# Attention phases of a fused attention and gated-MLP kernel placed one slot later against their start, with hand-set starts in the first block

## The chip, the cores and the metric

The kernel runs on 1 core of a Trainium2 chip. The metric is the device time of one execution in microseconds (us), median of three runs. The span in the profile is the part between the first and the last instruction.

## The reference

Three stages follow each other. The first is a gated linear attention with a 48x48 state for each of 32 heads (4 batches, 8 heads), over 768 positions; the second multiplies two projections and projects back; the third does the same with `h - tanh(h)`.

```python
f = 1.0 / (1.0 + np.exp(-f_logit))
for t in range(S):
    state = f[:, :, t, :, None] * state + np.einsum('bhd,bhe->bhde', k[:, :, t], v[:, :, t])
    y[:, :, t] = np.einsum('bhd,bhde->bhe', q[:, :, t], state)
...
x = ((x @ w_a) * (x @ w_b)) @ w_out        # 3072 x 384, d_ff 1536
h = x @ w_in                               # d_ff2 2048
return (h - np.tanh(h)) @ w_out2
```

## The kernel before

The order of all work is written out by hand; each engine executes its own queue in that order.

**Attention.** The sequence is cut into 12 chunks of 64 positions; with two halves of the batch this makes 24 steps. A step is a generator (`attn_step`) of twelve phases, named by the letters `FPRKVSMUYELD`: F sigmoid on ScalarE; P and R the forward and backward scans on VectorE; K three multiplies on VectorE that make KH, RA and RB (`L305` to `L307`); V two state copies on ScalarE; S the scores (`sc`) and transposes (`pk`) on TensorE; M the score evacuations RA, RB and KTS on ScalarE, with the causal masks on GpSimd; U the state update matmuls (`uu`) on TensorE, their sum T on VectorE (`L347`) and a multiply on GpSimd; Y the output matmuls (`yy`); E and L their evacuation to x on ScalarE and VectorE; D, in the last step of a block, six small transfers x<-y that complete x. Four steps make a block of 512 tokens; the kernel has 6 blocks. S needs the step's RA and RB, U needs KTS, and Y needs the first half of T, because its PSUM bank is the one that `uu` left.

**First MLP.** `moe1` runs 12 values of m over each block, three slots for each: after the `a` group of 9 matmuls and its ScalarE copy `asb` the first slot, after the `b` group, the VectorE product `gf` and its split the second, after the `y` group of the m before it the third. So slot s has `a` at s mod 3 = 0, `b` at 1 and `y` at 2, and a block has 36 slots. `gf` and `asb` have one buffer, and the `b` bank is free for the next m when `gf` has read it. While block jb is multiplied, the steps of block jb+1 are woven in: a table `OFF` and `LEAD` give each phase the slot behind which it is issued (`pulses`). All steps of blocks 1 to 5 use one working set, and the loads of the next step are issued at F and Y.

**Weight conversion.** The weights lie in HBM as 64-bit numbers. `w_tick` converts one 128x384 tile: three VectorE instructions (`L124` to `L126`), then a ScalarE copy and a GpSimd (later VectorE) subtraction (`L136`, `L138`). In the first block every slot 0 to 32 has one conversion, issued before that slot's phases, and the tile is used by the matmul group four slots later. Its input lies in three staging buffers `wst`, loaded from the sync queue. From block 1 on two conversions in nine slots prepare the third stage's weights (`CONV`), spilled to HBM.

**Second MLP.** From about 640 us `h` and `o` matmuls run with no attention beside them.

Of the kernel before, what the change touches and what calls it, by code (L numbers as in the profile page):

```python
# [28 lines left out]
def tile_kernel(ctx: ExitStack, tc: tile.TileContext, q, k, v, f, w_a, w_b, w_out, w_in, w_out2, l_fkq, l_tv, l_v, l_w1, l_w2, out):  # L29
# [16 lines left out]
    NSTEP = 2 * NC  # L46
    blocks = [4, 4, 4, 4, 4, 4]
    NBLK = len(blocks)
    first = [sum(blocks[:j]) for j in range(NBLK)]
    block_of = [j for j, n in enumerate(blocks) for _ in range(n)]  # L50
    PRO = blocks[0]
    SLOTS = 3 * MF
    LEAD = 6
    PHASES = "FPRKVSMUYELD"
    OFF = (0, 1, 2, 4, 5, 6, 6, 8, 9, 9, 10, 11)
    CONV = (3, 7)
    SEQ = ("lf0 lk0 lf1 lt0 lk1 lv0 lf2 lt1 lv1 lk2 w lf3 lt2 lv2 lk3 w lt3 lv3 w x x x x F0 P0 F1 R0 K0 x x lf4 lk4 x V0 S0 P1 M0 F2 "
           "R1 K1 U0 Y0 lt4 lv4 x V1 S1 P2 E0 F3 M1 R2 L0 K2 x U1 Y1 x V2 S2 P3 E1 M2 L1 R3 K3 x U2 Y2 x V3 S3 x x E2 M3 c L2 F4 c P4 "
           "x x U3 x Y3 x E3 L3 R4 c K4 V4")
    TW = 528  # L60

    const = ctx.enter_context(tc.tile_pool(name="const", bufs=1))
# [79 lines left out]
    def w_spill():  # L142
        name, m, wt = spilled.pop(0)
        nc.sync.dma_start(out=wsp[2 * m + "ip".index(name)], in_=wt.bitcast(F32))
# [21 lines left out]
    with tc.manual_schedule(), ExitStack() as p1:  # L166
# [64 lines left out]
        def t_of(i):  # L231
            return T[i if i < min(PRO, 4) else i % 2]

        def tv_of(i):
            return TV[i if i < min(PRO, 4) else i % 2]
# [4 lines left out]
        def load_t(i, sl):  # L240
            t = t_of(i)
            if i < PRO:
                nc.sync.dma_start(out=t[:, sl], in_=l_fkq[i, :, sl])
            else:
                for r0 in (0, 64):
                    nc.sync.dma_start(out=t[r0:r0 + D, sl], in_=l_fkq[i, r0:r0 + D, sl])

        def load_v(i):
            w = w_of(i)
            for ab, (vs, r0) in enumerate(((w.VS_A, 64), (w.VS_B, 0))):  # L250
                nc.sync.dma_start(out=vs[r0:r0 + 64], in_=l_v[i, ab])

        def load_tv(i):
            nc.sync.dma_start(out=tv_of(i), in_=l_tv[i])
# [21 lines left out]
        Y3 = {}  # L276
# [121 lines left out]
        pulses = []  # L398
        for jb in range(1, NBLK):
            for si in range(blocks[jb]):  # L400
                for p, o in enumerate(OFF):
                    at = (9 * si + o) * SLOTS // (9 * blocks[jb]) - LEAD
                    pulses.append((SLOTS * (jb - 1) + at, first[jb] + si, p))
        pulses.sort(key=lambda e: e[0])

        phase = [0] * NSTEP
# [1 line left out]
        def pulse(i, p):  # L408
            assert phase[i] == p
            phase[i] += 1  # L410
            if i >= PRO and p == 0 and i + 1 < NSTEP:
                load_t(i + 1, slice(0, 3))
                load_tv(i + 1)
            next(gens[i], None)
            if i >= PRO and PHASES[p] == "Y" and i + 1 < NSTEP:
                load_v(i + 1)
# [11 lines left out]
        def w_tick(upto):  # L428
            while nconv[0] < upto and (loaded or half):
                if loaded:  # L430
                    half.append(w_start(loaded.pop(0)))
                    w_fetch()
                if len(half) > 1 or not loaded or half[0][0] in "abo":
                    w_finish(half.pop(0))
                nconv[0] += 1
# [70 lines left out]
        for it in SEQ.split():  # L506
            if it == "c":
                w_tick(nconv[0] + 1)
            elif it == "w":
                w_fetch(len(loaded) + 1)  # L510
            elif it == "x":
                warm()
            elif it[0] == "l":
                i = int(it[2])
                if it[1] == "f":
                    load_t(i, slice(0, 1))
                elif it[1] == "k":
                    load_t(i, slice(1, 3))
                else:
                    (load_tv if it[1] == "t" else load_v)(i)  # L520
            else:
                i, p = int(it[1]), PHASES.index(it[0])
                if i >= PRO:
                    pulses.pop(0)
                pulse(i, p)
        for i in range(PRO):
            pulse(i, len(PHASES) - 1)
# [14 lines left out]
        for g, jb in enumerate(moe1(None)):  # L542
            slot = g % SLOTS
            if jb == 0:
                w_tick(min(NW1, npro + slot + 1))
            else:
                if g == SLOTS:
                    rot.update(n=3, conv=None)
                if spilled:
                    w_spill()  # L550
                if (g + LEAD) % (SLOTS // 4) in CONV and jb < NBLK - 1 or (jb == NBLK - 1 and slot == 0):
                    w_tick(min(nconv[0] + 1, NW2 + 1))
            while pulses and pulses[0][0] <= g:
                _, i, p = pulses.pop(0)
                pulse(i, p)
            if not pulses and not done:
                done = True
                nc.vector.tensor_reduce(r1, PMS.rearrange("p i u -> p (i u)"), mybir.AxisListType.X, ALU.min)
                nc.vector.tensor_scalar(r1, r1, P_MIN, None, ALU.is_ge)
            if jb == NBLK - 1:  # L560
                if slot == 2:
                    x2first.append(load_x2(0))
                elif slot > 2 and fills and len(fills) > 2 * MF2 + 3 - slot:
                    w_fill(*fills.pop(0))
# [37 lines left out]
        for i in range(NO * MF2 + LAG):  # L602
            g = None
            if i < NO * MF2:
                o, m = divmod(i, MF2)
# [196 lines left out]
```

## Time and profile before

| what | value |
|---|---|
| median of 3 runs | 997.63 us (997.12 to 998.8) |
| profiled execution | 997.97 us, span 996.3 us |
| TensorE (matmul) busy | 961.1 us, 96% of the span |
| VectorE, ScalarE, GpSimd busy | 620.4, 475.1, 123.3 us |
| mean granted TensorE clock | 0.983 |

The busy shares are averages over three regimes: the first some 40 us with four steps of attention alone, the first block with its conversions (to about 155 us), and the rest. The profiled execution lies 1.7 us above its own span, and 0.3 us above the median.

### The profile page before, as it was taken

The numbers are of one execution on the slowest core, as the hardware profiler recorded it, in microseconds if no ns is written. First come the engines' busy times: TensorE is split into PE (matmuls) and PEld (weight loads), VectorE is DVE, ScalarE is ACT, GpSimd is POOL, SyncE is SP. The second block draws the span as 40 slices with busy tenths as digits, with TensorE's granted clock in tenths as the row PEclk, the third lists the DMA queues.
The fourth block names the chain that finished last, engine by engine and source line by source line (L and its number), as shares of the span: only waits on it lengthen the run. The fifth ranks groups of instructions, "written<-read, shape, count | busy, mean of one in ns | idle before, by whom it ended". The sixth has DMA issues, their size and how long they took to land.

```text
span 996.3 us, 15895 instructions
## 1 busy us (share of the span) xinstructions
PE 961.1 (96%) x6155; PEld 773.3 (78%) x6155; DVE 620.4 (62%) x1045; ACT 475.1 (48%) x925; POOL 123.3 (12%) x144
## 2 busy tenths in 40 slices
PE   7879989999999999999999999999999999999997
PEld 4667767887887788887888888888888888888885
DVE  8787875666656566675552238666666666666663
ACT  4424443333433433343422137666666666666663
POOL 5456552000110010000100000000000000000000
PEclk9889989999999999999999999999999999999999
DMA  9456654545634554564228651020100100200001
GB/s 276 111 154 170 170 136 135 142 114 131 186 106 114 142 175 125 128 194 121 85 75 325 195 184 47 1 96 1 63 33 1 64 33 1 95 1 1 32 1 35
DMA packets 41172, 104.54 MB, mean 105 GB/s; under 512 B 5600, under 2 KB 8672, under 8 KB 41088
## 3 DMA queue, kind: packets, MB, share of 16 engines
q1 hardware_dynamic: 40368, 102.45, 34.8%
q10 hardware_dynamic: 720, 0.98, 0.5%
q8 instruction: 50, 0.82, 0.4%
q14 instruction: 34, 0.28, 0.1%
HBM read 74.71 MB, written 26.74 MB: 102 GB/s over the span
## 4 chain that ended last, share of the span: by engine, by line
PE 89%; DVE 7%; issue 1%; DMA 1%; ACT 1%; POOL 0%; DVEq 0%; ACTq 0%
PE o L164 20%; PE h L164 20%; PE b L164 15%; PE a L164 13%; PE y L164 13%; PE yy L357 2%; PE sc L319 2%; PE pk L323 1%; PE uu L339 1%; DVE cv L125 1%; PE sc L320 1%; DVE cv L124 1%; DVE PRE L293 1%; DVE RA L306 1%; DVE R L298 1%
## 5 line engine op out<-in xcount | busy, mean ns | idle before, releaser
L164 PE MATMUL h<-x,w_i 128*128 128x512 f32 x864 | 213.0, 391 | 0.0
L164 PE MATMUL o<-gh,w_p 128*128 128x512 f32 x576 | 194.7, 393 | 0.0
L164 PEld LDWEIGHTS h<-x,w_i 128*128 128x128 f32 x864 | 162.2, 188 | 36.4
L164 PE MATMUL b<-x,w_b 128*128 128x512 f32 x648 | 169.3, 407 | 0.0
L492 DVE TENSOR_TENSOR gf<-asb,b 128x512 f32<-128x512 f32 x72 | 49.4, 686 | 192.1 <-PE b L164 128.9
L164 PE MATMUL a<-x,w_a 128*128 128x512 f32 x648 | 164.5, 398 | 2.6 <-DMA x<-y 2.3
L164 PE MATMUL y<-gh,w_o 128*128 128x512 f32 x432 | 146.1, 393 | 0.0
L164 PEld LDWEIGHTS a<-x,w_a 128*128 128x128 f32 x648 | 120.4, 189 | 31.0 <-ACT gh L493 2.7
L164 PEld LDWEIGHTS b<-x,w_b 128*128 128x128 f32 x648 | 122.9, 195 | 26.2
L104 DVE SCALAR_TENSOR_TENSOR xu<-u,h 128x512 f32<-128x512 f32 x96 | 66.0, 688 | 111.8 <-ACT u L101 111.7
L164 PEld LDWEIGHTS o<-gh,w_p 128*128 128x128 f32 x576 | 108.2, 188 | 24.7
L101 ACT ACTIVATE u<-h 128x512 f32<-128x512 f32 x96 | 57.5, 599 | 132.7 <-PE h L164 132.0
L164 PE MATMUL o<-gl,w_p 128*128 128x512 f32 x288 | 113.1, 393 | 0.0
L487 ACT ACTIVATE asb<-a 128x512 f32<-128x512 f32 x72 | 43.0, 597 | 141.0 <-PE a L164 139.1
L493 ACT ACTIVATE gh<-gf 128x512 fp32r<-128x512 f32 x72 | 45.6, 633 | 125.9 <-DVE gf L492 125.7
L164 PEld LDWEIGHTS y<-gh,w_o 128*128 128x128 f32 x432 | 81.1, 188 | 18.2
L164 PE MATMUL y<-gl,w_o 128*128 128x512 f32 x216 | 84.8, 393 | 0.0
L105 DVE SCALAR_TENSOR_TENSOR v<-v,xu 128x512 f32<-128x512 f32 x96 | 66.4, 692 | 10.4 <-ACT v L102 0.5
L106 DVE SCALAR_TENSOR_TENSOR v<-v,v 128x512 f32<-128x512 f32 x96 | 66.5, 692 | 10.0
L102 ACT ACTIVATE v<-u,bias 128x512 f32<-128x512 f32 x96 | 69.6, 725 | 3.1
L103 ACT ACTIVATE v<-u,bias 128x512 f32<-128x512 f32 x96 | 68.1, 710 | 0.6 <-DVE gl L574 0.6
L574 DVE TENSOR_TENSOR gl<-v,gh 128x512 fp32r<-128x512 f32 x96 | 65.7, 684 | 0.2 <-ACT gh L573 0.2
(96 smaller groups left out, 1119.2 us busy)
## 6 DMA issues: line engine op xcount, KB each, us to landing
wst<-in_l_w_dram SPq DMA_DIRECT2D x68, 384.0 KB, 3.3
wsp<-wst SPq DMA_DIRECT2D x32, 384.0 KB, 2.4
T<-in_l_fkq_dram SPq DMA_DIRECT2D x38, 288.0 KB, 5.2
x<-xs SPq DMA_DIRECT2D x12, 768.0 KB, 5.3
w_i<-wsp SPq DMA_DIRECT2D x16, 384.0 KB, 3.6
w_p<-wsp SPq DMA_DIRECT2D x16, 384.0 KB, 3.6
TV<-in_l_tv_dram SPq DMA_DIRECT2D x24, 192.0 KB, 5.4
xs<-oh SPq DMA_DIRECT2D x18, 256.0 KB, 2.3
```

The costliest lines, as they stand in the source:

```text
L101: nc.scalar.activation(u, h, ACTF.Square, accum_out=total)
L102: nc.scalar.activation(v1, u, ACTF.Square, bias=bias1)
L103: nc.scalar.activation(v2, u, ACTF.Square, bias=bias2)
L104: nc.vector.scalar_tensor_tensor(xu, u, Q4, h, ALU.mult, ALU.mult)
L105: nc.vector.scalar_tensor_tensor(v1, v1, Q_Y1, xu, ALU.add, ALU.mult)
L106: nc.vector.scalar_tensor_tensor(v2, v2, Q_Y2, v1, ALU.add, ALU.mult)
L164: nc.tensor.matmul(dst, l_, r_, start=(first and i == 0), stop=(last and i == 2))
L319: nc.tensor.matmul(sc[64:128, u], KH[0:64, u], RA[0:64, u], start=True, stop=True)
L487: nc.scalar.activation(asb, pb, ACTF.Copy)
L492: nc.vector.tensor_tensor(gf, asb, pab[1], ALU.mult)
L493: nc.scalar.activation(gh, gf, ACTF.Copy)
L574: nc.vector.tensor_tensor(gl, g, gh.bitcast(F32), ALU.subtract)
```

## The change

The phases S to D move one place away from F (`OFF`), and `LEAD` grows by one. For blocks 2 to 5 this leaves S to D in their slots, issues F, P, R, K and V one slot earlier, and the conversions too, which use the same `LEAD`. For the four steps of block 1, woven into the first block, a table `FIRST` gives the slot of F by hand: F moves from -6, 3, 12, 21 to -5, 4, 12, 20, so that S moves from slots 0, 9, 18, 27 to 2, 11, 19, 27, and U from 2, 11, 20, 29 to 4, 13, 21, 29. V of step 4 moves from the prologue into slot 0. The load of the next step's `TV` moves from F to K.

```diff
-    LEAD = 6
+    LEAD = 7
+    FIRST = (-5, 4, 12, 20)
     PHASES = "FPRKVSMUYELD"
-    OFF = (0, 1, 2, 4, 5, 6, 6, 8, 9, 9, 10, 11)
+    OFF = (0, 1, 2, 4, 5, 7, 7, 9, 10, 10, 11, 12)
...
-           "x x U3 x Y3 x E3 L3 R4 c K4 V4")
+           "x x U3 x Y3 x E3 L3 R4 c K4")
...
-                    at = (9 * si + o) * SLOTS // (9 * blocks[jb]) - LEAD
-                    pulses.append((SLOTS * (jb - 1) + at, first[jb] + si, p))
+                    at = FIRST[si] + o if jb == 1 else SLOTS * (jb - 1) + 9 * si - LEAD + o
+                    pulses.append((at, first[jb] + si, p))
...
                 load_t(i + 1, slice(0, 3))
+            if i >= PRO and PHASES[p] == "K" and i + 1 < NSTEP:
                 load_tv(i + 1)
```

TensorE at step 5's scores, before. The first row is `a` of m=3, `pk` ends S; rows of `sc` stand for sixteen.

```order
L164 MATMUL a<-x,w_a_886 128x512 x9
L319 MATMUL sc<-RA,KH 64x64
...
L320 MATMUL sc<-RB,KH 64x64
L323 MATMUL pk<-ident,KH 128x128 x4
L164 MATMUL b<-x,w_b_911 128x512 x9
L164 MATMUL y_867<-gh,w_o_937 128x512
```

The same place after the change, from `a` of m=3 to the first state matmul of step 5.

```order
L165 MATMUL a<-x,w_a_859 128x512 x9
L165 MATMUL b<-x,w_b_905 128x512 x9
L165 MATMUL y_840<-gh,w_o_936 128x512
...
L324 MATMUL pk<-ident,KH 128x128 x4
L165 MATMUL a<-x,w_a_955 128x512 x9
L165 MATMUL b<-x,w_b_981 128x512 x9
L340 MATMUL uu_1109<-TV_183,KTS 64x48 x2
```

The scores now stand behind `b` and `y`; `uu` stands behind a `b` group, where it stood behind a `y` group.

ScalarE at step 5's evacuations, before: the weight copies are those of slots 8 and 9.

```order
L136 ACTIVATE w_a_959<-wc 128x384
L310 ACTIVATE VS_A<-ST_131 64x8x48
L311 ACTIVATE VS_B<-ST_131 64x8x48
L487 ACTIVATE asb<-a 128x512
L136 ACTIVATE w_b_983<-wc 128x384
L327 ACTIVATE RA<-sc 64x512
L327 ACTIVATE RB<-sc 64x512
L332 ACTIVATE KTS<-pk 128x512
L493 ACTIVATE gh<-gf 128x512
```

The same place after the change; the weight copies are those of slots 10 and 11.

```order
L137 ACTIVATE w_o_1009<-wc 128x384
L137 ACTIVATE w_a_1028<-wc 128x384
L328 ACTIVATE RA<-sc 64x512
L328 ACTIVATE RB<-sc 64x512
L333 ACTIVATE KTS<-pk 128x512
L489 ACTIVATE asb<-a 128x512
L137 ACTIVATE w_b_1077<-wc 128x384
```

RA, RB and KTS now stand behind the copy of slot 11 and ahead of `asb` of m=4; before, `asb` of the running m stood ahead of them.

## Rows read from the trace of the kernel before

**Rows 1.** Busy time by stretch: us, PE, PEld, DVE, ACT, POOL, clock, DMA share, GB/s

```profile
81.00:110.00 29.00, 24.71 (x214) 19.90 (x207) 24.11 (x43) 12.09 (x24) 17.50 (x16) 0.94 0.58 159
430.00:520.00 90.00, 90.00 (x700) 72.22 (x698) 52.34 (x100) 32.79 (x64) 8.46 (x12) 1.00 0.38 114
```

**Rows 2.** Groups of VectorE instructions, 41.6 to 150.9 us; last number idle before

```profile
L492 DVE TENSOR_TENSOR gf<-asb,b 128x512 f32<-128x512 f32 x11 | 7.5, 686 | 20.4 <-PE b L164 13.2 <-POOL RA L328 5.4 <-POOL w_b L138 1.8
L293 DVE TENSOR_TENSOR_SCAN PRE<-F,D 128x520 f32<-128x520 f32 x4 | 4.9, 1232 | 0.0
L306 DVE TENSOR_TENSOR RA<-T,PRE 64x512 f32<-64x512 f32 x3 | 4.4, 1474 | 0.0
```

**Rows 3.** TensorE's waits, 0 to 160 us: total, times, longest

```profile
PE sc L319 <- DVE RA L306: 17.3, 5, 4.0
```

**Rows 4.** Timeline around the scores of step 6

```profile
101.37 0.30 PE L319 MATMUL sc<-RA,KH 64*64 64x64 f32 x2 [3.95 <-DVE RA L306]
107.33 0.69 DVE L492 TENSOR_TENSOR gf<-asb,b 128x512 f32<-128x512 f32 x1 [1.69 <-PE b L164]
107.93 0.56 DVE L124 TENSOR_SCALAR cv<-wst 128x384 int32<-128x384 int32 x1
109.78 0.56 DVE L124 TENSOR_SCALAR cv<-wst 128x384 int32<-128x384 int32 x1
111.51 0.62 DVE L347 TENSOR_TENSOR T<-uu,ST 128x192 f32<-128x192 f32 x2
```

**Rows 5.** Timeline of VectorE, first instruction of slot 0's conversion

```profile
41.58 0.56 DVE L124 TENSOR_SCALAR cv<-wst 128x384 int32<-128x384 int32 x1
```

**Rows 6.** Chain that ended last, 133 to 191 us: start, us, what

```profile
133.47 3.23 PE b L164 x9
...
150.42 0.56 DVE wc L126
...
151.07 4.35 DMA x<-y
155.55 3.54 PE a L164 x9
...
183.41 2.08 PE b L164 x9
...
187.56 0.61 PE uu L339 x32
...
190.46 1.08 PE yy L357 x32
```

**Rows 7.** Timeline of ScalarE, evacuations of step 6

```profile
105.95 0.53 ACT L136 ACTIVATE w_b<-wc 128x384 fp32r<-128x384 f32 x1
107.61 0.58 ACT L332 ACTIVATE KTS<-pk 128x512 f32<-128x512 f32 x1
112.27 0.60 ACT L487 ACTIVATE asb<-a 128x512 f32<-128x512 f32 x1
```

**Rows 8.** TensorE by stretch: us, busy, granted clock, DMA share, GB/s

```profile
50.70:52.60 1.90, 0.06 (x1) 1.00 0.57 142
55.00:57.50 2.50, 2.50 (x7) 0.54 0.71 184
```

**Rows 9.** Timeline in block 1 and at the change to block 2

```profile
228.83 0.58 ACT L332 ACTIVATE KTS<-pk 128x512 f32<-128x512 f32 x1
232.25 0.68 PE L339 MATMUL uu<-TV,KTS 64*64 64x48 f32 x32
240.06 2.19 SPq L380 DMA_DIRECT2D x<-y  x3
245.74 0.68 DVE L305 TENSOR_TENSOR KH<-T,R 128x512 f32<-128x512 f32 x1
246.68 2.22 PE L164 MATMUL a<-x,w_a 128*128 128x512 f32 x9
```

**Rows 10.** Landing of the staged weights' transfers, 40 to 150 us

```profile
DMA to landing us min/median/max: 3.0/3.2/7.0
```

## Prediction

> **What bounds the kernel now.** I read the busy table by stretch first. From 430 to 520 us TensorE is busy in all of its 90 us at a clock of 1.00 [rows 1], and it is so in every stretch from 160 us to the end of the first MLP: there the step costs what its matmuls cost, and a phase moved within a gap of another engine changes nothing. In the first block it is different: 24.71 of 29 us busy, clock 0.94, with VectorE at 24.11 of 29 [rows 1]. The waits name the place: TensorE waited five times, 17.3 us in total, at the first score matmul for VectorE's RA [rows 3].
>
> That is half of a circle. VectorE's groups show the other half: between the first and the last conversion of the block it stood idle 20.4 us, all of it in front of `gf`, waiting for the `b` group [rows 2]. One turn, at step 6: `sc` waits 3.95 us for RA and starts at 101.37; then come `sc`, `pk` and `b`, so `gf` of m=6 starts at 107.33 after 1.69 us of idling [rows 4], and the next `gf` waits again. Then VectorE works without a pause until the next RA, and TensorE waits. Whoever is late makes the other wait, alternately. (Two of the releasers in the row of `gf` are GpSimd's; what `gf` needs is `asb` and `b`, and `b` ended right before.)
>
> So I do the accounting on VectorE. Its conversion of slot 0 starts at 41.58 [rows 5], that of slot 32 ends at 150.98 (150.42 and 0.56), and the next block's first `a` starts at 155.55 [rows 6]: a stretch of 109.4 us, of which 20.4 are idle [rows 2] and 89.0 are work in queue order, and a tail of 4.6 us (ScalarE's copy, then the transfers x<-y of 4.35 us [rows 6]). The change alters none of the 89.0 except what it reorders. What it saves is what it takes out of the 20.4.
>
> **The first block after the change.** S of steps 4 and 5 stands two slots later, of step 6 one, while K of step 7 stands one slot earlier. Prices: a conversion takes VectorE 1.85 us (107.93 to 109.78), `gf` 0.60 (107.33 to 107.93), T 0.62 [rows 4], P 1.23 [rows 2]; a matmul group 2.08, `uu` 0.61, `yy` 1.08 [rows 6].
>
> Does S still wait in a way that VectorE feels? From the end of `gf` of m=2, VectorE does two conversions and K (about 6.9 us at the durations of step 6) and step 5 is ready; TensorE, from the end of that same `b`, has `y`, `a`, `b`, `y` to do, 8.3 us. As VectorE reaches that `gf` 1 to 2 us late, S waits about 1 us at most and VectorE not at all. It then stays behind TensorE, and each `gf` finds its `b` finished, with these exceptions, where something else is late:
>
> - `asb` of m=1 and m=4 now stands in ScalarE's queue behind RA, RB and KTS of steps 4 and 5, and these behind the weight copy of slots 2 and 11. From the end of that conversion the five copies take 2.9 us: copy to the end of KTS 2.24 (105.95 to 108.19) and 0.60 of `asb` [rows 7], plus 0.04. VectorE has one conversion of 1.85 meanwhile: idle 1.05 at each of two `gf`, 2.1.
> - The V copies of step 6 stand ahead of `asb` of m=6: 0.3.
> - At step 6 KTS is ready 2.28 us after the conversion of slot 19, so `uu`, now in slot 21, waits some 2 to 3 us for ScalarE. `uu` and `b` of m=7 end 4.97 after that conversion; VectorE, with two conversions, T and P, arrives after 5.5. Nothing at full clock.
> - At step 7 `uu`, `a`, `yy`, `b` of m=10 end 8.13 after the conversion of slot 27, VectorE, with `gf`, three conversions, T and P, arrives after 7.9 to 8.0: 0.2.
>
> These are 2.6 us. The clock adds to them. TensorE's idling of 1.9 us from 50.70 to 52.60 is followed by a granted clock of 0.54, the lower of its two levels (1.2 of 2.4 GHz) but for the part where it changes [rows 8], and a `b` after such a wait takes 3.23 us where others take 2.08 [rows 6]. The new waits of `uu` are 2 to 3 us long, so I count the lower clock behind each: 1.15 us more for the next group. Behind steps 4 and 5 VectorE is late enough to hide it; behind 6 and 7 it makes the two items 0.6 and 1.3. The sum is 2.1 + 0.3 + 0.6 + 1.3 = 4.3 us of idle left.
>
> One item more: R of step 8 is issued before the conversion of slot 32, which ends the stretch, where it stood behind it: about 1.6 us are added (a scan like P's 1.23 [rows 2] behind two small instructions on 8 columns, taken as 0.2 each).
>
> Saved: 20.4 - 4.3 - 1.6 = 14.5 us. Without any lower clock it would be 16.2.
>
> **What else moves, at nothing.** V of step 4 goes from the prologue to slot 0; ScalarE waits for the conversion there. The load of `TV` goes from F to K, four slots later; its reader U comes more than ten slots after. Both pass only staged weight loads on the sync queue. Those are asked for when the conversion three before has read the buffer, so with `gf` and two conversions between them they have 4.3 us, against a landing of 3.2 in the median and 7.0 at worst [rows 10]. If that cover were gone, VectorE would wait in the conversions.
>
> In blocks 2 to 5 S to D keep their slots. The conversion now stands at S, its ScalarE copy ahead of RA: 0.5 us in a queue where KTS ends at 229.41 and `uu` starts at 232.25 [rows 9], 2.8 us of cover. K stands a slot earlier, ahead of its `gf`, which comes some 1.5 us late; the `b` bank that it frees is wanted two groups, S and more later. At the change of block the transfers x<-y are issued at 240.06 and need some 4.4 us; `a` starts at 246.68 [rows 9], 2.2 us to spare, and the `T` load that stood just ahead of them now stands further ahead. So nothing there.
>
> **How fast VectorE is itself** is the term that the trace leaves open, since it will run with GpSimd for a larger share of the time. RA took 1.47 us in this stretch [rows 2], while KH, the same kind of multiply, took 0.68 in block 1, where GpSimd is nearly idle [rows 9]. If the scans and all three multiplies of each step were held as RA is, up to 0.8 each for the three that are not held now, four steps would cost 7 to 9 us; if none were held, 4 us would be gained. I take today's durations, because the multiplies still follow conversions, whose GpSimd subtractions they meet now too.
>
> The Trainium skill (SBUF — State Buffer, section "SBUF: two separate sides") says that VectorE and GpSimd share a port pair by an exclusive lock, which a VectorE instruction with two SBUF inputs takes, and that the loser waits for the whole instruction. RA's 1.47 us agrees. By that rule alone, with GpSimd busy in most of the shortened block, I would expect the held case, and about 991 us.
>
> **Forecast and rivals.** The sum stands against the profiled execution's own 997.97 (span 996.3 and 1.7 around it), 0.3 above the median: 997.97 - 14.5 = 983.5.
>
> - Likeliest, VectorE-bound first block with a few microseconds of idle left: 980 to 988, chance 0.58.
> - VectorE itself slower (multiplies and scans held, or staged loads late by a microsecond in some conversions): 14.5 less 4.5 to 12, so 988 to 995.6, about 991. For it: GpSimd has the same work in less time. Against: RA is held already [rows 2], so GpSimd's share is in today's work. 0.20.
> - More saved, no lower clock and multiplies held less: below 980. 0.08.
> - The wait moves, no gain: `uu` waits for KTS behind conversions, and `asb` behind them makes `gf` late by as much as before. This needs 4 to 5 us of idle per step; the queue from conversion to `asb` is 2.9 long, with 1.85 of VectorE's work beside it. Then 998; 0.05.
> - Slower: the conversion at S in blocks 2 to 5 makes KTS late for `uu` in each of 16 steps. An idling of 1.9 and the lower clock's 1.15 would cost 3 us a step, 48 in all, less the 14.5: about 1031. It decides when RA, RB and KTS come over 2.8 us later than now; the copy put ahead takes 0.5 and its input is ready. 0.09 for this and smaller cases of its kind.
>
> A change of 0.2% (2 us) is about what a measurement of this kernel tells from none. Faster by more: 0.58 + 0.20 + 0.08 = 0.86; within it 0.05; slower 0.09. The range leaves out no more than the slower and the unchanged cases and the edges: 980.0 to 991.5, where the held multiplies stand.
>
> **What would show it.** Right: the next block's first `a` near 141 us, VectorE's idle before `gf` near 5 us in the block, no wait of 4 us of `sc` for RA, and in its place waits of `uu` for KTS of 2 to 3 us with a lower clock behind them. Wrong: RA, RB or the scans longer than now; idle in front of the conversions for staged loads; any TensorE wait after 160 us.

## The result

The changed kernel takes 987.67 us (median of 4 runs, 986.92 to 988.12) against 997.5 us (997.12 to 998.8) for the kernel before: a ratio of 0.9902, 95% interval 0.9885 to 0.992, or 9.8 us less. The profiled execution's span went from 996.3 to 985.4 us, and the mean granted clock from 0.983 to 0.993.

All of it lies ahead of 160 us. By stretch, with the columns of [rows 1] (us, PE, PEld, DVE, ACT, POOL, clock, DMA share, GB/s), the changed kernel shows:

```profile
81.00:110.00 29.00, 25.03 (x217) 19.91 (x217) 24.30 (x42) 11.22 (x22) 15.29 (x16) 0.99 0.62 163
430.00:520.00 90.00, 90.00 (x644) 72.61 (x644) 50.20 (x93) 31.85 (x60) 6.48 (x9) 1.00 0.39 120
```

From 430 to 520 us TensorE is busy without a pause as before, and so it is in every stretch from 160 us to the end of the first MLP. The second block's first `a` starts at 146.18, where it started at 155.55 [rows 6], and the `b` behind it at 150.17, where the trace of before has it at 161.06. That last difference, 10.9 us, is the whole difference of the spans.

TensorE's waits from 0 to 160 us after the change, as total, times, longest:

```profile
PE uu L340 <- ACT KTS L333: 10.9, 7, 2.5
PE sc L320 <- DVE RA L307: 4.4, 3, 2.9
...
PE a L165 <- ACT asb L489: 2.2, 3, 1.7
```

The 17.3 us of `sc` for RA [rows 3] are 4.4. Not all of the 17.3 lay in the first block: from 41 to 160 us the kernel before has 11.8 us in 3 waits, and the changed kernel 1.5 in 2. `uu` for KTS has taken their place.

VectorE's groups from its first conversion (42.31) to its last (142.99), with the columns of [rows 2]:

```profile
L494 DVE TENSOR_TENSOR gf<-asb,b 128x512 f32<-128x512 f32 x11 | 7.5, 680 | 4.3 <-ACT asb L489 2.4 <-PE b L165 1.9
L299 DVE TENSOR_TENSOR_SCAN R<-F,D 128x520 f32<-128x520 f32 x4 | 6.8, 1692 | 0.1
L294 DVE TENSOR_TENSOR_SCAN PRE<-F,D 128x520 f32<-128x520 f32 x4 | 5.0, 1242 | 4.8 <-POOL ST L351 4.8
L308 DVE TENSOR_TENSOR RB<-T,PRE 64x512 f32<-64x512 f32 x3 | 3.5, 1153 | 0.1
...
L307 DVE TENSOR_TENSOR RA<-T,PRE 64x512 f32<-64x512 f32 x3 | 2.8, 948 | 0.0
```

`gf` idles 4.3 us, where it idled 20.4. But P, the scan that writes PRE, now idles 4.8 us, where [rows 2] has 0.0. The timeline at step 6 shows why:

```profile
103.16 0.68 PE L340 MATMUL uu<-TV,KTS 64*64 64x48 f32 x32 [2.46 <-ACT KTS L333]
...
104.46 0.61 DVE L348 TENSOR_TENSOR T<-uu,ST 128x192 f32<-128x192 f32 x2
105.18 1.01 POOL L139 TENSOR_TENSOR w_b<-wc,w_b 128x384 fp32r<-128x384 f32 x1 [0.27 <-ACT w_b L137]
106.15 0.85 POOL L351 TENSOR_TENSOR ST<-T,PRE 128x384 f32<-128x384 f32 x1
107.03 1.24 DVE L294 TENSOR_TENSOR_SCAN PRE<-F,D 128x520 f32<-128x520 f32 x1 [1.95 <-POOL ST L351]
```

T is done at 105.1; the next thing on VectorE is P of step 7. GpSimd still has to multiply T by a factor that it reads from PRE (`ST`), and that multiply stands behind the subtraction of the conversion. PRE has one buffer, so P waits 1.95 us. Before the change two slots lay between T and P.

The end of the block, in the chain of waits (start, us, what), to set beside [rows 6]:

```profile
142.44 0.56 DVE wc L127
143.01 0.02 issue
143.03 0.53 ACT w_o L137
143.56 0.24 ACTq L381
143.80 0.04 issue
143.84 0.60 ACTq L381
...
145.13 0.61 ACT asb L489
145.74 0.44 issue
146.18 2.32 PE a L165 x9
```

From the last conversion to `a` it is 3.2 us (4.6 before). The profile puts the wait of `a` down to `asb`, which stands behind three DMA issues on ScalarE's queue, but `asb` had ended 0.44 us earlier. The landing times of the six transfers x<-y, from 130 to 150 us, fit better:

```profile
DMA to landing us min/median/max: 2.4/2.5/3.0
```

The longest, 3.0, is that of the first transfer on ScalarE's queue, issued at 143.09; it lands at 146.1, and `a` starts at 146.18. Before the change the same transfer took 4.35 and `a` started as shortly behind it [rows 6]. So `a` most likely still waits for that landing, and the 1.4 us are a faster landing. `a` then takes 2.32, where it took 3.54 [rows 6].

### The profile page after: what moved, and what is told of

Its sections match the earlier page's. It is cut to its first block, busy times and chain, and to the rows that moved or that the text cites. A ratio compares the mean times of both kernels' runs of the same rounds, so it can differ in the third digit from the quotient of the medians.

```text
span 985.4 us, 15896 instructions
## 1 busy us (share of the span) xinstructions
PE 954.8 (97%) x6155; PEld 766.5 (78%) x6155; DVE 629.5 (64%) x1045; ACT 475.5 (48%) x925; POOL 119.1 (12%) x144
## 4 chain that ended last, share of the span: by engine, by line
PE 87%; DVE 7%; issue 2%; ACT 2%; POOL 1%; DMA 0%; ACTq 0%; DVEq 0%; POOLq 0%
PE o L165 20%; PE h L165 20%; PE a L165 13%; PE b L165 13%; PE y L165 13%; PE yy L358 2%; PE sc L320 2%; DVE cv L126 2%; DVE cv L125 1%; PE uu L340 1%; DVE wc L127 1%; PE pk L324 1%; DVE R L299 1%; DVE RB L308 1%; DVE gf L494 0%
## 5 line engine op out<-in xcount | busy, mean ns | idle before, releaser
L165 PE MATMUL a<-x,w_a 128*128 128x512 f32 x648 | 166.8, 402 | 2.6 <-ACT asb L489 2.2
L165 PE MATMUL b<-x,w_b 128*128 128x512 f32 x648 | 163.2, 396 | 0.0
L165 PEld LDWEIGHTS b<-x,w_b 128*128 128x128 f32 x648 | 119.0, 188 | 25.1
```

The lines of the kernel that those rows point to most:

```text
L165: nc.tensor.matmul(dst, l_, r_, start=(first and i == 0), stop=(last and i == 2))
```

## The experiments

Each experiment was timed beside runs of the kernel before on the same chip (997.7 to 998.2 us in the median). Differences from the changed kernel are taken between medians. Beside the changed kernel the kernel before had 997.5, so up to 0.7 us of such a difference need not come from the edit.

**e1: the carried state's factor read from another buffer.**

```
-  nc.gpsimd.tensor_tensor(st, w.T1, pend.to_broadcast(...), ALU.mult)
+  nc.gpsimd.tensor_tensor(st, w.T1, PMS[:, i].unsqueeze(2).to_broadcast(...), ALU.mult)
```

> The changed kernel, but GpSimd's multiply for the carried state (ST) takes its factor from PMS, the scan with its lower limit applied, and not from PRE, so that the next step's P, which writes PRE, no longer has GpSimd in its way; the engines' orders stay the same. The changed kernel's VectorE stands idle 4.8 us in front of four P scans in the first block, all put down to that multiply. Theory 1, that wait lies on the path because VectorE sets the first block's length: the idle in front of P goes and the kernel takes 4 to 5 us less, 983 to 984 us. Rival, the wait is hidden: VectorE then only comes earlier to the same b groups and stands idle in front of gf instead (4.3 us there now, then 7 to 9), and the time stays at 987 to 988 us.

982.78 us (ratio 0.985, interval 0.983 to 0.987): 4.9 below the changed kernel. VectorE's groups from 42.26 to 138.07:

```profile
L494 DVE TENSOR_TENSOR gf<-asb,b 128x512 f32<-128x512 f32 x11 | 7.5, 681 | 3.0 <-ACT asb L489 2.4 <-PE b L165 0.6
...
L294 DVE TENSOR_TENSOR_SCAN PRE<-F,D 128x520 f32<-128x520 f32 x4 | 5.7, 1417 | 0.0
```

The wait of P is gone and does not come back in front of `gf`; the stretch is 95.8 us, where the changed kernel has 100.7. Theory 1 holds: the 4.8 us lie on the path.

**e4: the same edit in the kernel before.**

> The kernel before with the same edit as in the first experiment: the multiply for ST takes its factor from PMS. In the kernel before P stands two slots behind T and shows no idle time in front of it. Theory 1, the wait on GpSimd was made by the change: no difference here, 997 to 998.5 us. Rival, reading PMS in place of PRE is faster by itself, or frees VectorE in another way: 1 us or more is gained here too, and the first experiment's gain has to be read less that.

997.58 us (ratio 0.9989, 0.9977 to 1.0001). No gain that can be told from none, so e1's 4.9 us are the price of a wait that the change made, not of a slow read.

**e2 and e3: each half of the change alone.** In e2 the four steps of block 1 get the changed slots, the rest keeps the old ones; in e3 the other way about.

```
 e2   LEAD = 6;  FIRST = (-5, 4, 12, 20)
      for p, o in enumerate(OFF1 if jb == 1 else OFF):
      PHASES[p] == ("K" if block_of[i] == 1 else "F")      # load of TV
 e3   LEAD = 7;  FIRST = (-6, 3, 12, 21), old offsets and V4 for block 1
```

> The kernel before, with the changed kernel's slots for the four steps woven into the first block alone (the table FIRST, the offsets, V of step 4 in slot 0, and the load of TV at K for those steps); blocks 2 to 5 and the conversions there as before. Theory 1, all of the gain comes from the first block: within 0.5 us of the changed kernel, 987 to 988 us, and the first a of the second block near 146 us. Rival, a part comes from blocks 2 to 5 or from the change at the block's end: 989 us or more, with TensorE waits after 160 us that the changed kernel does not have.

> The changed kernel with the first block's four steps put back to their old slots, blocks 2 to 5 and the conversions there as changed. Theory 1, the move in blocks 2 to 5 is worth nothing, since TensorE is busy there all the time: 997 to 998.5 us, as before. Rival, the earlier P, R and K, or the conversion at S, help or hurt there: a change of 2 us or more against the kernel before (at 0.1 us a step it would be 1.6 us over 16 steps).

e2 takes 986.73 us (0.9881, 0.9864 to 0.9898), e3 999.01 us (1.0007, 0.9994 to 1.002). The gain is the first block's alone; the move in blocks 2 to 5 is worth nothing that shows. In e2 R of step 8 stays behind the last conversion, which ends at 142.08, 0.9 earlier than in the changed kernel, but the end of the block is the old one:

```profile
142.17 4.32 DMA x<-y
146.48 0.14 issue
146.62 3.83 PE a L166 x9
```

The landing of 4.32 us is as long as before the change; in e3, with the other half, the same transfer took 3.27. But e2's profiled execution is the slowest of its five (989.05 us), and in the medians no longer tail shows. So these profiles do not show that the slots of blocks 2 to 5, or the loads that move with them, shorten the tail.

**e5: a costlier conversion.** The last of the three VectorE instructions is done twice.

```
     nc.vector.scalar_tensor_tensor(c, lo, 29, t, ALU.logical_shift_right, ALU.bitwise_or)
+    if name in "abo":
+        nc.vector.scalar_tensor_tensor(c, lo, 29, t, ALU.logical_shift_right, ALU.bitwise_or)
```

> The changed kernel with the last VectorE instruction of a weight conversion of the first MLP done twice; nothing else differs and the values stay. That is 33 instructions of 0.55 us in the first block and 3 ahead of it. Theory 1, VectorE sets the first block's length: each of the 33 is added to it, 18 us, less what the 4.3 us of idle in front of gf and the 4.8 us in front of P take up, so 9 to 20 us more than the changed kernel, 997 to 1008 us. Rival, TensorE with ScalarE's evacuations sets the length and VectorE only follows: TensorE waited some 17 us in the block (10.9 for KTS), of which little would change, and the addition is under 5 us, below 993 us.

1002.98 us (1.0057, 1.0042 to 1.0073): 15.3 more than the changed kernel. VectorE's groups from 43.28 to 157.86:

```profile
L129 DVE SCALAR_TENSOR_TENSOR wc<-wst,cv 128x384 int32<-128x384 int32 x33 | 18.3, 554 | 1.1
L496 DVE TENSOR_TENSOR gf<-asb,b 128x512 f32<-128x512 f32 x11 | 7.5, 679 | 1.8 <-PE b L167 0.9 <-ACT asb L491 0.8
...
L296 DVE TENSOR_TENSOR_SCAN PRE<-F,D 128x520 f32<-128x520 f32 x4 | 5.0, 1238 | 3.9 <-POOL ST L353 3.9
```

Of 18.3 us added to VectorE's queue, 13.9 lengthen the stretch (114.6 against 100.7), and 3.4 are taken from the two idle times. So VectorE's queue sets most of the length of the first block; e6 shows what else counts.

**e6: ScalarE's copies behind its evacuations.** In the first block the copy and the subtraction of a conversion are issued behind the slot's phases.

```
-  w_tick(min(NW1, npro + slot + 1))
+  w_tick(min(NW1, npro + slot + 1), late=True)      # converts, doesn't copy yet
   while pulses and pulses[0][0] <= g: ...
+  while jb == 0 and half:
+      w_finish(half.pop(0))                         # copy and subtraction
```

> The changed kernel, but in the first block ScalarE's copy and GpSimd's subtraction of a conversion are issued behind the phases and the a copy of the slot, not ahead of them, so that RA, RB, KTS and asb no longer stand behind the copy of their own slot, which waits for VectorE. Theory 1, VectorE sets the length: the waits of uu for KTS (10.9 us of TensorE over 7 times) shorten by some 5 us, but the time falls only by VectorE's idle that hangs on ScalarE, at most the 2.4 us of gf behind asb: 985 to 988 us. Rival, those waits of TensorE are part of the length: 5 to 8 us less, 980 to 983 us.

979.67 us (0.9818, 0.9805 to 0.9832): 8.0 below the changed kernel, where theory 1 had allowed 2.4. VectorE's groups from 42.19 to 137.79:

```profile
L494 DVE TENSOR_TENSOR gf<-asb,b 128x512 f32<-128x512 f32 x11 | 7.4, 677 | 0.5 <-PE b L165 0.5
L294 DVE TENSOR_TENSOR_SCAN PRE<-F,D 128x520 f32<-128x520 f32 x4 | 6.8, 1691 | 1.9 <-POOL ST L351 1.9
```

The price that theory 1 gave was wrong, its mechanism not altogether. It counted `gf` behind `asb` alone. In the trace `gf`'s idle falls by 3.8 us (4.3 to 0.5): the 2.4 behind `asb`, and most of the 1.9 behind a `b` that came late because its `uu` had waited for KTS. To that extent the rival is right: TensorE's wait did reach VectorE. P's wait falls by 2.9, since GpSimd's multiply now stands ahead of the subtraction, and P's own scans grow by 1.8. That makes 4.9 of the 5.1 by which the stretch is shorter. Most of the rest is the tail: `a` starts 1.4 us behind the last conversion (139.16), where it took 3.2.

**e8 and e9: e6 in two parts.** e8 puts only the copy of slot 32, the block's last, behind the phases (`late=slot >= 32`), e9 all the others (`late=slot < 32`).

> The changed kernel, with the copies behind the slot's phases in slot 32 alone, the last conversion of the first block: the six transfers x<-y at the block's end and the a copy behind them no longer stand behind a ScalarE copy that waits for that conversion. In the changed kernel TensorE stands idle 1.73 us there before the second block's first a, put down to asb. Theory 1, the tail is a term of its own: 1.7 us less, 985.5 to 986.5 us, and a follows y without a wait. Rival, a then waits for the transfers themselves (2 us of landing) or for the conversion: no change, 987 to 988 us.

> The changed kernel with the copies behind the slot's phases in slots 0 to 31, and the last one, of slot 32, where the changed kernel has it. With copies behind in all slots VectorE's stretch from the first to the last conversion was 95.6 us against the changed kernel's 100.7, and the tail to a 1.4 against 3.2. Theory 1, the two add: the stretch stays 95.6 and the tail comes back, 981 to 982.5 us, 1.5 to 2 more than with all copies behind. Rival, the gain hangs on the whole queue or mostly on the last slot: under 980.5, or over 984 us.

e8 takes 985.41 us (0.9883, 0.9866 to 0.99), 2.3 below the changed kernel, and e9 982.41 us (0.9843, 0.9829 to 0.9857), 5.3 below. Together 7.5, of the 8.0 of e6: the medians add. e8's share is the less certain one: two of its five runs (987.25 and 987.44) lie among those of the changed kernel. ScalarE at the block's end in e8:

```profile
138.63 2.00 ACTq L381 DMA_DIRECT2D x<-y  x3
142.32 0.53 ACT L137 ACTIVATE w_o<-wc 128x384 fp32r<-128x384 f32 x1 [3.87 <-DMA x<-y]
142.75 0.58 ACT L489 ACTIVATE asb<-a 128x512 f32<-128x512 f32 x1
```

The three transfers are issued at 138.63, where the changed kernel issued them at 143.09 behind a copy that waited 3.86 us for the conversion; `a` starts at 143.38, as soon as `y` and `asb` end. e9's stretch is 95.6 us as in e6. Its profiled execution is the slowest of its six (987.27 us) and lost its time in the tail: the first transfer on ScalarE's queue, issued at 139.14, took 4.9 us to land, and `a` started 0.1 us behind it, at 144.16. In the changed kernel the same transfer, issued at the same place, took 3.0.

**e10: the copies behind, in the kernel before.** The edit of e6, with the old slots.

> The kernel before, with its old slots, and the copies behind the slot's phases in the first block. Theory 1, what bound that kernel was TensorE and VectorE waiting for each other at the scores (17.3 us of sc for RA, 20.4 us of VectorE in front of gf), in which ScalarE's copies have no part: the circle stays, only the tail of 4.6 us to the second block's first a and the lower clock behind it can fall, 3 to 5 us, 992.5 to 995 us. Rival, the copies ahead of the evacuations were the cause, and the slots could have stayed: 8 us or more, under 990 us, with VectorE's idle in front of gf well below 20 us.

995.64 us (0.9977, 0.9966 to 0.9987): 2.1 less than the kernel before, under the 3 to 5 expected, and far from the rival's 8. VectorE from its first to its last conversion:

```profile
L492 DVE TENSOR_TENSOR gf<-asb,b 128x512 f32<-128x512 f32 x11 | 7.6, 687 | 21.0 <-PE b L164 21.0
```

The idle in front of `gf` is all there (20.4 in [rows 2]). The circle of that kernel does not hang on ScalarE's copies; the change of slots had to come first, and then the copies were worth 8 us.

**e7: both edits, in the changed kernel** (e1 and e6).

> Both edits, that of the first experiment (ST takes its factor from PMS) and the copies issued behind the evacuations. Theory 1, VectorE's idle is what remains to be had: 982.8 us as in the first experiment, less at most the 2.4 us of gf behind asb, so 980.5 to 983 us. Rival, the two do not add because with P early VectorE waits for b groups that wait for KTS, and these fall too: more than 3 us below the first experiment, under 979.5 us.

976.35 us (0.9784, 0.9771 to 0.9798), the fastest version here, 11.3 below the changed kernel. As in e6, theory 1's price is too small, the rival's number (under 979.5) the nearer one. VectorE from 42.67 to 134.89, and TensorE's stretch from 41 to 160 us:

```profile
L494 DVE TENSOR_TENSOR gf<-asb,b 128x512 f32<-128x512 f32 x11 | 7.5, 678 | 0.5 <-PE b L165 0.5
...
L294 DVE TENSOR_TENSOR_SCAN PRE<-F,D 128x520 f32<-128x520 f32 x4 | 5.1, 1283 | 0.0
```

```profile
41.00:160.00 119.00, 109.50 (x885) 87.17 (x886) 107.02 (x185) 54.98 (x109) 65.70 (x61) 1.00 0.67 180
```

VectorE has 0.5 us of idle left in front of `gf` and P in its 92.2 us, and the granted clock is 1.00 throughout (0.96 in the changed kernel over the same 119 us).

## Why the prediction was right, point by point

It gave 983.5 us in a range of 980.0 to 991.5; 987.67 lies in the range and in the likeliest case (980 to 988), at its upper edge. The span shrank by 10.9 us, where 14.5 were forecast, and the `a` that was to start near 141 us started at 146.18. The terms, from the two traces:

| term | forecast, us | measured, us |
|---|---|---|
| idle in front of `gf`, 20.4 before | 4.3 left | 4.3 left |
| wait of P for GpSimd's ST | 0 | 4.8 |
| VectorE's work, 89.0 before | 90.6 | 91.6 |
| start of the first conversion | 41.58 | 42.31, 0.7 later |
| last conversion to `a`, 4.6 before | 4.6 | 3.2 |
| `a` to the next `b`, 5.5 before | 5.5 | 4.0 |

14.5 - 4.8 - 1.0 - 0.7 + 1.4 + 1.5 = 10.9.

The last two terms, 2.9 us, were in no part of the forecast, and they hide more than half of the wait that it missed. Without them the time would have been near 990.6, still in the range but outside the likeliest case; that it fell there is luck.

- **What bounds the kernel** was right. e5 shows VectorE's queue setting most of the first block, and e3 that blocks 2 to 5 give nothing that shows. It was not the whole: by e6 TensorE's waits for KTS reach VectorE too, through a late `b`.
- **The circle of `sc` and `gf`** was right: the waits of 4 us for RA are gone from the block, and e10 shows that without the new slots the 20 us stay. No run moves S alone, apart from V of step 4 and the loads.
- **The step that failed** is the walk through step 6: "VectorE, with two conversions, T and P, arrives after 5.5". T and P were counted as neighbours on VectorE with nothing between them. Between them stands GpSimd's ST, which reads what P overwrites. It waits for T and stands behind a subtraction of 1.01 us. The four waits of P are 0.23, 1.94, 1.95 and 0.69 us; the two long ones are at steps 5 and 6, where no conversion stands between T and P. The order of VectorE showed that U had come to stand right ahead of P; the buffer that both use was not asked for. e1 and e4 show the price (4.9 us) and that the change made it.
- **The items of the 4.3 us** were forecast as 1.05, 1.05, 0.3, 0.6 and 1.3 for m = 1, 4, 6, 7 and 10, and came as 0.99, 0.99, 0.37, 0 and 1.92. The queue on ScalarE behind a conversion was read right to a tenth of a microsecond. The last two are off in opposite directions, so that the sum of 4.3 came out is in part luck.
- **The lower clock** was counted behind each of four waits of `uu`. The waits were 0.84, 2.46, 2.46 and 2.40 us. Behind the first and the third the granted clock stayed at 1.00, behind the second and the fourth it fell (0.69 and 0.62 in the next 3 to 4 us) towards the lower level, 1.2 of 2.4 GHz. The third and the fourth:

```profile
101.00:104.00 3.00, 0.84 (x33) 0.79 (x34) 2.69 (x6) 2.95 (x7) 2.61 (x5) 1.00 0.58 147
104.00:108.00 4.00, 4.00 (x45) 3.13 (x45) 2.05 (x4) 1.05 (x3) 2.72 (x3) 1.00 0.99 240
...
125.00:128.30 3.30, 0.90 (x7) 0.39 (x5) 3.04 (x6) 2.41 (x6) 2.40 (x3) 1.00 0.78 211
128.30:132.00 3.70, 3.70 (x40) 3.02 (x41) 3.40 (x8) 1.91 (x4) 3.63 (x5) 0.62 0.66 166
```

  Two waits of the same length, with TensorE about as idle, and different clocks behind them: what decides is not in these rows. The 0.6 at m=7 did not come: the clock was full, and P's wait of 1.95 us right ahead of that `gf` would have covered it as well. In e1, without that wait of P, the clock behind a wait of 2.43 was full too, and `gf` did not idle there, as the forecast says ("Nothing at full clock"). A full clock is also the last term of the table: `a` at the change of block ran at full clock after 1.73 us of idling, where before it was slow after 2.3.
- **VectorE itself slower**, the rival at 991, did not happen in sum: scans of R, 1.24 to 1.69, and RB, 0.69 to 1.15, became slower, KH and RA faster; with PMS, the small instruction ahead of R, it is about 0.8 us net, the most part of the 1.0 in the table. The rule of the Trainium skill (SBUF — State Buffer, "SBUF: two separate sides") on the lock between VectorE and GpSimd agrees with single rows, below; the expectation of 991 us that was drawn from it took every one of these instructions as the loser, and here they lose by turns.
- **The tail** was taken as unchanged. It shrank with the landing of one transfer, 3.0 us after its issue for 4.35 before. Other profiles have 4.32 (e2), 3.27 (e3) and 4.9 (e9) for it, and what decides is not shown: the change also moves the loads of T and TV against these transfers, and no run moves them alone. e8 shows that some 2 us more lay there (2.3 in the medians), in the place of a copy in ScalarE's queue ahead of DMA issues that did not need it.
- **Nothing in blocks 2 to 5**, the cover for KTS, the loads, and V of step 4 in slot 0 at no cost: e2 and e3 bear it out in sum, to within 2 us; the slower rival at 1031 has nothing for it.

## What to carry to other kernels

When a phase is moved, list for each engine not only what its new neighbours take but what they share: a buffer with one copy that a third engine still reads makes two neighbours wait for that engine's whole queue. A wait that costs nothing in one order becomes the next bound in another, so an edit that is worth little now (e4, e10) may be worth several microseconds after the move (e1, e6). And what stands in a queue ahead of a DMA issue is part of the transfer's time.

## What the runs showed of the hardware that was not expected

VectorE's scans and multiplies and GpSimd's subtractions hold each other up instruction by instruction, and the one that starts later pays. The three VectorE instructions of a conversion do not show it: they take 0.55 to 0.56 us in the mean, before and after the change. Rows of the changed kernel, first of P and a subtraction, then of a subtraction and R:

```profile
56.06 1.24 DVE L294 TENSOR_TENSOR_SCAN PRE<-F,D 128x520 f32<-128x520 f32 x1 [0.23 <-POOL ST L351]
56.47 1.65 POOL L139 TENSOR_TENSOR w_a<-wc,w_a 128x384 fp32r<-128x384 f32 x1 [0.44 <-ACT w_a L137]
...
111.14 1.02 POOL L139 TENSOR_TENSOR w_o<-wc,w_o 128x384 fp32r<-128x384 f32 x1 [0.26 <-ACT w_o L137]
111.19 2.07 DVE L299 TENSOR_TENSOR_SCAN R<-F,D 128x520 f32<-128x520 f32 x1
```

The scan that starts first takes its 1.24 us and the subtraction, elsewhere 1.02, takes 1.65; where the subtraction starts 0.05 us ahead, the scan takes 2.07. e6 turned this against P: with `ST` issued ahead of the subtraction, the subtraction starts just ahead of P, and two of its four P scans took 2.03 us and the others 1.36 and 1.35, which gave back 1.8 of the 2.9 us won at the wait.
